# Two-chunk attention visits, two-bank PSUM tiles and a sliced second matmul in a kernel of blocked linear attention followed by a two-layer ELU network

## The chip, the cores and the metric

The kernel runs on one core of one Trainium2 chip. The metric is the device time of one execution in microseconds (us). A profiled execution also gives a span, from its first to its last instruction; here the span is about 1.8 us below the time.

## The reference, cut to what matters

For each of 4 sequences and 8 heads of width 64, attention runs over 768 positions in blocks, with a state per head that decays by a head's own lambda:

```python
intra = (qb @ kb.T * Dmask) @ vb                 # inside a block, masked by lam ** (i - j)
inter = (qb * lam_pow) @ kv_state                # from the blocks before
out_block = intra + inter
kv_state = lam_block * kv_state + (kb * rev_pow).T @ vb
# then, on x = the 3072 tokens x 512 features of out:
h = x @ w_in                                     # 512 -> 2048
g = where(h > 0, h, exp(min(h, 0)) - 1)          # ELU
y = g @ w_out                                    # 2048 -> 512
```

Both kernels use blocks of 128 positions. One block of one sequence with all 8 heads is a *chunk*; there are 24 chunks, six of each sequence. Four chunks (the same block of the four sequences) make a *tile* of 512 tokens. Chunks 0 to 3 feed tile 0, chunks 4 to 7 tile 1, and so on.

## The kernel before

Engines are called PE (matrix), DVE (vector), ACT (scalar), POOL (GpSimd) and SP (sync). A chunk goes through five stages, and the names of their PSUM tiles are the names in the profile: T (`psT`, 8 transposes of q and k), S (`psS`, 8 score matmuls, then DVE multiplies by the mask into `P`), O (`psO`, output, then DVE scales it into `xt`), U (`psU`, the state's update) and the state's own update `st`. A tile's first layer is 16 steps of four matmuls (`psH`), each followed by `e` and `r` on ACT and `g` on DVE; the second layer is 64 matmuls (`psM`).

```python
def att_U(g):                       # one chunk
    ...                             # 8 matmuls into pu
    for hh in range(2):
        r = slice(hh * 64, (hh + 1) * 64)
        if c == 0:
            nc.scalar.copy(out=new[r, :, r], in_=pu[r]); continue
        for hp in range(HP):        # HP = 4: eight pieces of 64 x 64 per chunk
            h = 2 * hp + hh
            nc.vector.scalar_tensor_tensor(
                out=new[r, hp, r], in0=old[r, hp, r], scalar=up[r, h : h + 1],
                in1=pu[r, hp, :], op0=ALU.mult, op1=ALU.add)
# ... cut: T, S, O of one chunk each, in one-bank PSUM tiles ...

# the first tile: T(j), S(j-1), O(j-2) of its four chunks
# then one step per first-layer block; one chunk's stages are placed among them:
for t in range(1, NT):
    for i in range(TS[t]):
        base = (t - 1) * NF + ([1, 4, 8, 11][i] if t == 1 else [-2, 2, 6, 10][i])
        at(base, att_T, g);     at(base, att_kd, g)
        at(base + 2, att_S, g); at(base + 2, att_U, g)
        at(base + 3, att_O, g)
for t in range(NT):
    for n in range(NF):             # NF = 16
        er = mm1(t, n)              # 4 matmuls, exp and relu
        for f in slots.get(t * NF + n, []): f()
        elu(t, n, *er)
        if t > 0: ...               # 4 matmuls of the second layer of tile t - 1
```

All loads but lambda's are issued on POOL's software queue and cast to 16 bits on the way. So a step holds eight 512-column matmuls, except in tile 0, whose steps hold four: its second layer runs wholly beside tile 1.

## Time and profile before

| | before |
|---|---|
| time, median of the first 3 runs | 249.97 us (249.71 to 250.82) |
| span of the profiled run (its time was 248.66) | 246.9 us |
| first PE work | 5.00 us |
| first `psH` of tile 0 | 23.15 us |
| first `psH` of tile 1 | 63.35 us |
| last matmul ends | 242.84 us |

The page of the kernel before: the span, the busy time of each engine, then rows that cut the span into 40 slices of about 6.2 us (busy share in tenths; PEclk is the granted clock of PE in tenths).

```profile
span 246.9 us, 4269 instructions
PE 217.1 (88%) x1664; PEld 107.1 (43%) x1664; DVE 163.9 (66%) x353; ACT 137.7 (56%) x265; POOL 51.7 (21%) x55
...
PE   0375748866999999999999999999999999999993
...
DVE  6347493999979877977977897787447644444210
...
PEclk9999995999999999999999999999999999999999
```

The average of 88% hides two regimes. From the eleventh slice on, PE is full; before, it is often idle, and DVE is nearly full from the eighth slice (43 us) to the eleventh (to 68 us). In the seventh slice (37.05 to 43.22 us) the granted clock of PE is 0.52. Only what happens before 65 us looks as if better overlap could save it.

Three of its groups of instructions (count, total busy us, mean ns of one, idle time before them):

```profile
L329 DVE SCALAR_TENSOR_TENSOR g<-e,r 128x512 f16<-128x512 f32 x96 | 65.8, 688 | 47.7 <-ACT r L325 47.2
...
L247 DVE TENSOR_TENSOR P<-psS,mask 128x512 f16<-128x512 f32 x48 | 30.8, 683 | 2.2 <-PE psS L242 1.9
L273 DVE SCALAR_TENSOR_TENSOR st<-st,up,psU 64x64 f16<-64x64 f16 x128 | 27.8, 279 | 0.2
```

The state's 128 small pieces cost 279 ns for 64 columns, where a `g` does 512 columns in 688 ns: the small ones are mostly fixed cost (an estimate: 448 columns more cost 409 ns, so 64 columns would be some 58 of the 279 ns).

What PE waited for (us in all, times, longest), and the busy times in a stretch of tile 0 (window, length, then busy us of PE, PEld, DVE, ACT, POOL, then clock, DMA share, GB/s):

```profile
PE psT L207 <- DMA qn<-in_q_dram: 8.4, 3, 5.0
PE psU L262 <- DVE st L273: 3.7, 1, 3.7
PE psU L262 <- ACT kT L216: 2.9, 2, 1.7
```

```profile
23.15:63.35 40.20, 28.27 (x264) 14.38 (x264) 31.20 (x72) 21.95 (x44) 20.56 (x20) 0.92 2.27 176
42.00:62.00 20.00, 15.18 (x159) 7.83 (x158) 18.80 (x46) 10.80 (x21) 10.27 (x9) 0.97 2.78 162
```

The second of these windows shows DVE busy for 18.8 of 20 us: there DVE sets the pace, with the four chunks of tile 1 beside tile 0's ELUs. The timeline of PE (start us, length us, what, and in brackets the idle time before it and what ended it) shows the start of tile 0, then one steady stretch of four steps:

```profile
23.15 3.25 PE L315 MATMUL psH<-xt,wi 128*128 128x512 f16 x8 [0.78 <-DVE xt L299]
...
84.70 1.04 PE L341 MATMUL psM<-wo,g 128*128 128x512 f16 x4
...
89.47 1.03 PE L315 MATMUL psH<-xt,wi 128*128 128x512 f16 x4
90.43 0.40 PE L242 MATMUL psS<-qT,kT 64*128 64x128 f16 x8
90.76 0.32 PE L262 MATMUL psU<-vn,kd 128*64 128x64 f16 x8
91.01 1.04 PE L341 MATMUL psM<-wo,g 128*128 128x512 f16 x4
...
93.41 1.04 PE L341 MATMUL psM<-wo,g 128*128 128x512 f16 x4
```

The first eight matmuls take 0.41 us each where four take 0.86 us in the steady part (0.216 each); the granted clock reads 1.00 there, and 0.50 at 40.34 us, where eight take 3.20 us. From 84.70 to 93.41 is one period with one chunk: 8.71 us, of which the 32 big matmuls are 6.91 and one chunk's visit is 1.8.

### The profile page before, as it was taken

The numbers are of one execution on the slowest core, as the hardware profiler recorded it, in microseconds if no ns is written. First come the engines' busy times: TensorE is split into PE (matmuls) and PEld (weight loads), VectorE is DVE, ScalarE is ACT, GpSimd is POOL, SyncE is SP. The second block draws the span as 40 slices with busy tenths as digits, with TensorE's granted clock in tenths as the row PEclk, the third lists the DMA queues.
The fourth block names the chain that finished last, engine by engine and source line by source line (L and its number), as shares of the span: only waits on it lengthen the run. The fifth ranks groups of instructions, "written<-read, shape, count | busy, mean of one in ns | idle before, by whom it ended". The sixth has DMA issues, their size and how long they took to land.

```text
span 246.9 us, 4269 instructions
## 1 busy us (share of the span) xinstructions
PE 217.1 (88%) x1664; PEld 107.1 (43%) x1664; DVE 163.9 (66%) x353; ACT 137.7 (56%) x265; POOL 51.7 (21%) x55
## 2 busy tenths in 40 slices
PE   0375748866999999999999999999999999999993
PEld 0243324433445445545544554454454444444441
DVE  6347493999979877977977897787447644444210
ACT  4510735645675576476566656755765757666200
POOL 8996455166551031000000000000000000000000
PEclk9999995999999999999999999999999999999999
DMA  8999999999999979110110111011101101111212
GB/s 51 140 170 171 181 190 206 177 156 147 148 145 170 131 50 123 44 45 0 45 44 9 37 42 43 2 44 45 42 3 42 42 1 45 42 42 42 79 51 85
DMA packets 83924, 20.20 MB, mean 82 GB/s; under 512 B 76096, under 2 KB 80960, under 8 KB 83904
## 3 DMA queue, kind: packets, MB, share of 16 engines
q0 software_dynamic: 80160, 13.63, 87.0%
q1 hardware_dynamic: 3600, 6.17, 6.9%
q8 instruction: 13, 0.21, 0.4%
q10 hardware_dynamic: 144, 0.13, 0.2%
q14 instruction: 7, 0.06, 0.1%
HBM read 27.27 MB, written 6.29 MB: 136 GB/s over the span
## 4 chain that ended last, share of the span: by engine, by line
PE 78%; DVE 12%; DMA 3%; POOL 3%; ACT 2%; issue 1%; POOLq 0%; DVEq 0%
PE psM L341 35%; PE psH L315 31%; PE psT L207 3%; DVE P L247 3%; DMA kn<-in_k_dram 3%; PE psO L286 3%; DVE st L273 3%; DVE g L329 3%; PE psS L242 2%; PE psU L262 2%; DVE xt L299 2%; PE psO L293 2%; POOL qn L73 1%; DVE r L323 1%; DVE kd L223 1%
## 5 line engine op out<-in xcount | busy, mean ns | idle before, releaser
L315 PE MATMUL psH<-xt,wi 128*128 128x512 f16 x384 | 101.2, 388 | 2.5 <-DVE xt L299 1.4
L329 DVE SCALAR_TENSOR_TENSOR g<-e,r 128x512 f16<-128x512 f32 x96 | 65.8, 688 | 47.7 <-ACT r L325 47.2
L320 ACT ACTIVATE e<-psH 128x512 f32<-128x512 f32 x96 | 57.4, 598 | 71.8 <-PE psH L315 65.9
L341 PE MATMUL psM<-wo,g 128*128 128x512 f16 x384 | 96.3, 380 | 0.0
L315 PEld LDWEIGHTS <-wi 128*128 128x128 f16 x384 | 37.4, 100 | 47.9 <-issue 6.8
L325 ACT ACTIVATE r<-psH 128x512 f16<-128x512 f32 x91 | 53.9, 592 | 0.0
L341 PEld LDWEIGHTS <-g 128*128 128x128 f16 x384 | 34.3, 98 | 36.6
L247 DVE TENSOR_TENSOR P<-psS,mask 128x512 f16<-128x512 f32 x48 | 30.8, 683 | 2.2 <-PE psS L242 1.9
L273 DVE SCALAR_TENSOR_TENSOR st<-st,up,psU 64x64 f16<-64x64 f16 x128 | 27.8, 279 | 0.2
L207 PE MATMUL psT<-ident,qn 128*128 128x128 f16 x96 | 10.4, 237 | 10.7 <-DMA qn<-in_q_dram 8.4
L216 ACT COPY kT<-psT 128x512 f16<-128x512 f16 x24 | 14.6, 607 | 9.2 <-DVE qT L212 9.2
L299 DVE TENSOR_TENSOR xt<-psO,qs 128x512 f16<-128x512 f32 x24 | 16.5, 688 | 4.0 <-PE psO L293 2.9
L73 POOL DMA_DIRECT2D qn<-in_q_dram x13 | 14.7, 1131 | 17.5 <-PE psT L207 10.6
L286 PE MATMUL psO<-P,vn 128*64 128x128 f16 x192 | 15.2, 242 | 3.2 <-DVE xt L299 1.7
L73 POOL DMA_DIRECT2D vn<-in_v_dram x13 | 14.6, 1122 | 12.8 <-PE psO L293 7.7
L73 POOL DMA_DIRECT2D kn<-in_k_dram x13 | 14.6, 1123 | 8.0 <-DVE g L329 3.1
L286 PEld LDWEIGHTS <-vn 128*64 128x64 f16 x192 | 10.6, 119 | 11.6 <-issue 11.6
L214 ACT COPY qT<-psT 128x512 f16<-128x512 f16 x20 | 11.8, 591 | 5.7 <-PE psT L207 5.6
L223 DVE TENSOR_TENSOR kd<-kn,ks 128x512 f16<-128x512 f16 x20 | 13.7, 683 | 1.5 <-PE psU L262 1.4
L207 PEld LDWEIGHTS <-qn 128*128 128x128 f16 x96 | 7.6, 104 | 15.9 <-DMA qn<-in_q_dram 8.9
L207 PE MATMUL psT<-ident,kn 128*128 128x128 f16 x96 | 10.4, 238 | 2.7 <-DMA kn<-in_k_dram 2.7
L361 ACT COPY osb<-psM 128x512 f32<-128x512 f32 x12 | 7.1, 591 | 9.6 <-PE psM L341 9.6
(37 smaller groups left out, 90.8 us busy)
## 6 DMA issues: line engine op xcount, KB each, us to landing
out_dram<-osb SPq DMA_DIRECT2D x23, 256.0 KB, 2.0
qn<-in_q_dram POOLq DMA_DIRECT2D x11, 256.0 KB, 12.6
kn<-in_k_dram POOLq DMA_DIRECT2D x11, 256.0 KB, 12.4
vn<-in_v_dram POOLq DMA_DIRECT2D x11, 256.0 KB, 12.5
wo<-in_moe_w_out_dram POOLq DMA_DIRECT2D x4, 512.0 KB, 16.8
wi<-in_moe_w_in_dram POOLq DMA_DIRECT2D x2, 512.0 KB, 12.9
wi<-in_moe_w_in_dram POOLq DMA_DIRECT2D x3, 256.0 KB, 9.5
qn<-in_q_dram POOLq DMA_DIRECT2D x2, 128.0 KB, 4.0
```

Of the source, the lines that this page charges most:

```text
L73: nc.gpsimd.dma_start(out=dst, in_=src[b : b + n, :, rows].rearrange("b h p d -> p (b h) d"))
L207: nc.tensor.transpose(pt[:, j, hp, :], in_=nat[:, 2 * hp : 2 * hp + 2, :], identity=ident16[:])
L223: nc.vector.tensor_tensor(out=dst, in0=heads(kn, g), in1=ks[:].unsqueeze(2).broadcast_to([128, H, 64]), op=ALU.mult,)
L247: nc.vector.tensor_tensor(out=P[:, hh], in0=ss[hh][:], in1=mask[:, hh], op=ALU.mult)
L273: nc.vector.scalar_tensor_tensor(out=new[r, hp, r], in0=old[r, hp, r], scalar=up[r, h : h + 1], in1=pu[r, hp, :], op0=ALU.mult, op1=ALU.add,)
L286: nc.tensor.matmul(po[r, hp, :], lhsT=v_of(g, 2 * hp + hh), rhs=P[:, hh, hp, :], start=True, stop=(c == 0), skip_group_check=True,)
L299: nc.vector.tensor_tensor(out=xt[t][:, :, i * L : (i + 1) * L], in0=po[:], in1=qs[:], op=ALU.mult)
L315: nc.tensor.matmul(pH[:], lhsT=wi[:, kk, j * 128 : (j + 1) * 128], rhs=xt[t][:, kk, :], start=(kk == 0), stop=(kk == HP - 1),)
L320: nc.scalar.activation(e[:], pH[:], AF.Exp)
L325: nc.scalar.activation(r[:], pH[:], AF.Relu)
L329: nc.vector.scalar_tensor_tensor(out=gt[t][:, n, :], in0=e[:], scalar=-1.0, in1=r[:], op0=ALU.add, op1=ALU.min)
L341: nc.tensor.matmul(pm[:], lhsT=gt[t][:, n, i * L : (i + 1) * L], rhs=wo_t[wo_at[n][0]][:, wo_at[n][1], :], start=(n == 0), stop=(n == NF - 1),
```

## The change

The intent is to empty the time before 65 us. Six parts:

1. q, k, v of chunk 0 are loaded uncast on the hardware queues of SP and ACT; DVE casts q and k, ACT casts v.
2. Attention visits two chunks at once (T of two, S of two, then O and U of two), with PSUM tiles of two banks.
3. The state's update is one POOL multiply and one DVE add of 512 elements per half of the partitions and pair of chunks, in place of 16 pieces.
4. Tile 0's second layer starts in slices: one slice per step late in tile 0, then 16 steps without a first layer, the rest beside tile 1.
5. The order of the first four chunks is written out, with nine matmuls that only keep PE busy (`warm`).
6. The state's zeroes move from DVE to POOL; four ELUs of tile 0 move part of their work from ACT to DVE; the load buffers go from 6 to 12.

```diff
+    for w, src, e in (("q", q, nc.sync), ("k", k, nc.scalar), ("v", v, nc.sync)):
+        e.dma_start(out=first[w][:], in_=src[0, :, 0:L].rearrange("h p d -> p h d"))
-    NB = 6
+    NB = 12
 ...
+    for w, ts in (("q", qn), ("k", kn)):
+        nc.vector.tensor_copy(ts[0][:, 0:H, :], first[w][:])
 ...
+        nc.scalar.copy(vn[0][:, 0:H, :], first["v"][:])
 ...
+    def att_tmp(g, eng="p"):
+        for hh in range(2):
+            e.tensor_tensor(out=tmp[r], in0=old[r, :, :, r],
+                in1=up_p[r].unsqueeze(1).unsqueeze(3).broadcast_to([64, 2, HP, 64]), op=ALU.mult)
+    def att_st(g):
         for hh in range(2):
             if c == 0:
-                nc.scalar.copy(out=new[r, :, r], in_=pu[r])
-            for hp in range(HP):
-                nc.vector.scalar_tensor_tensor(out=new[r, hp, r], in0=old[r, hp, r], ...)
+                (nc.scalar.copy if hh else nc.vector.tensor_copy)(out=new[r, :, :, r], in_=pu[r])
+            else:
+                nc.vector.tensor_tensor(out=new[r, :, :, r], in0=tmps[g][r], in1=pu[r], op=ALU.add)
 ...
+    def visit(g, s0, s1, s2, s3=None):
+        at(s0, att_T, g, 2, "q"); at(s0, att_T, g, 2, "k")
+        ...
+        at(s1, att_S, g); at(s1, att_S, g + 1)
+        at(s1, att_mask, g); at(s1, att_mask, g + 1)
+        at(s2, att_tmp, g)
+        at(s2, att_O, g, 2); at(s2, att_U, g); at(s2, att_X, g, 2); at(s2, att_st, g)
+    for g, vs in [(4, (('A', 11), ('A', 13), ('A', 15))), (6, (('B', 7), ('B', 10), ('B', 13))),
+                  (8, ((1, 0), (1, 2), (1, 4))), (10, ((1, 8), (1, 10), (1, 12))), ...
+    steps = [(('A', 0), (0, 0), []), ...              # 'A': tile 0's first layer
+             (('A', 10), (0, 10), [(0, 0, 0), (0, 1, 0)]), ...   # with slices of its second
+             (('B', 0), None, []), ... (('B', 15), None, [(0, 0, 15), (0, 1, 15)]),
+             ((1, 0), (1, 0), [(0, 2, 0), (0, 2, 1)]), ...       # two per step beside tile 1
+             ((2, 0), (2, 0), [(1, 0, 0), (1, 0, 1), (1, 0, 2), (1, 0, 3)]), ...
```

(Marks of cuts: three dots. The names `A`, `B` are steps of tile 0 with and without a first layer.)

## The prediction

> **What bounds the kernel now.** The span is 246.9 us (timed runs about 3 us more). The timeline shows two regimes. From 64.9 us to its last matmul at 242.8 us PE never stops: four 512-column matmuls start every 0.86 us, one attention chunk adds 1.79 us (8.70 us per four steps, 6.91 of it matmuls); 4.05 us of copy and store follow. So counted, PE needs about 207 us in all; 246.9 - 207 - 4 leaves about 36 us of idle or half-rate PE, all before 65 us: 5.0 us until the first q lands; to 23.15 us loads and eviction chains of tile 0's four chunks; then DVE (busy 18.8 of the 20 us of window 42 to 62) holds tile 0, with tile 1's attention between its first matmuls. The list of waits shows PE waiting 8.4 us on q loads, 3.7 on st, 2.9 on kT. At 23.15 and 40.3 us eight first-layer matmuls take 3.2 us (0.41 each against 0.216)[...].
>
> **What the change does.**
> - Chunk 0 comes over hardware queues; the other loads issue 2.6 us earlier (three issues of 0.88). [...]k of chunks 2 and 3 landed at 14.7, I expect about 13. Adds two DVE casts of about 0.4 us, one ACT copy of 0.5.
> - State updates: DVE did 16 pieces (2 x 1.75 us) per pair of chunks; now two adds of 512 elements, about 0.6 us each. Saves about 2.2 us of DVE per pair, 17 us in all. The decay multiply goes to POOL, behind load issues.
> - Wider ops save only fixed cost: mask 1.28 to about 1.2 us per chunk.
> - Eight memsets (2.1 us) leave DVE; four ELUs of tile 0 move work from ACT to DVE.
> - Tile 0's first matmul runs with little attention in between; its second starts in slices, spread over tile 0, a phase without first matmul, and tile 1. PE work is unchanged but for nine warming matmuls.
>
> **Arithmetic.** Steady part: PE-bound, no gain. Head: first PE at about 4.5 us; first-layer matmul at about 18.5 (was 23.15). Up to tile 1's first matmul PE then has 13.8 (first layer) + 6.9 (half of tile 0's second) + 7.7 (updates, attention of tile 1) = 28.3 us; I add 1 us cold clock, 1.5 us DVE queueing (early steps need about 10.4 us of DVE against 8 of PE), 1.5 us mask and eviction waits in the phase without first matmul. Tile 1 begins at about 51 us. Loads agree: at the 170 to 200 GB/s of the profile's row, the last wo lands near 46 us. Remaining PE work 172.8 us, 0.5 us of stalls in tile 1, 4.05 tail: span 228, time **231 us**, range 226 to 238. Chances: faster 0.95, within 2% 0.04, slower 0.01.
>
> **What would show it.** Tile 0's first psH matmul at 18 to 19 us; tile 1's near 51; PE unbroken from about 60 us, same 0.86 us per four; DVE busy about 15 us lower; st below 12 us; the same 4 us end.
>
> **What would make it wrong.** Hardware loads of 256-byte rows slow the others, so tile 0 and the late wo slices wait. Two rotating two-bank buffers serialise T, S, O and U. DVE stalls on POOL's multiply, queued behind loads. Cold clock through tile 0. If all overlaps better than I add up, 226.

18.5 + 28.3 + 1 + 1.5 + 1.5 = 50.8, about 51, and 51 + 172.8 + 0.5 + 4.05 is about 228. The 1 us of cold clock (PE at half rate) and the two 1.5 us are allowances; each of the two slow stretches of eight matmuls in the kernel before lost about 1.5 us (3.2 - 8 x 0.216). The times for the adds and the copy on ACT fit what that kernel shows from start to start: 0.60 us for 512 columns back to back on DVE (94.58, 95.18, 95.78 us), 0.49 on ACT (84.24, 84.73); the time for the casts fits DVE's copies of `qT`, 0.42 us. From start to end, in the changed kernel, an add took 0.68 us, the two casts on DVE 0.43 and 0.79, the cast on ACT 0.60.

## The result, and the profile after

| | before | after | difference |
|---|---|---|---|
| time, median of 4 | 250.39 us (249.71 to 251.27) | 229.44 us (229.26 to 229.47) | -20.95 |
| span of the profiled run | 246.9 | 227.5 | -19.4 |
| first PE work | 5.00 | 7.27 | +2.27 |
| first `psH` of tile 0 | 23.15 | 20.79 | -2.36 |
| tile 0 to the first `psH` of tile 1 | 40.20 | 33.69 | -6.51 |
| from there to the end of the last matmul | 179.49 | 169.20 | -10.29 |
| tail | 4.06 | 3.82 | -0.24 |

The ratio is 0.916 (95% interval 0.9127 to 0.9193), faster. A ratio here is the mean time of one kernel's runs over the mean of the other's of the same rounds, so not quite the ratio of the medians that are quoted. Executions over 1.5% slower than the fastest of the same kernel are left out of the means. The profiled run of before was 1.7 us faster than its median, which is why the spans differ by less than the times.

The last two phases of the table must be read together. Of tile 0's 64 second-layer matmuls, 32 (32 x 0.216 = 6.9 us) moved from beside tile 1 into tile 0's phase. So tile 0's phase became 6.5 us shorter although it took in 6.9 us of PE work, and the later phase lost those 6.9 us and 3.4 us besides.

The page and the groups after:

```profile
span 227.5 us, 4119 instructions
PE 209.0 (92%) x1673; PEld 105.4 (46%) x1673; DVE 148.3 (65%) x193; ACT 135.9 (60%) x244; POOL 75.2 (33%) x75
...
PE   0488969989998999999999999999999999999993
...
DVE  2549885798876999997887667647537544534110
...
PEclk9999988999999999999999999999999999999999
...
L379 DVE SCALAR_TENSOR_TENSOR g<-e,r 128x512 f16<-128x512 f32 x92 | 68.6, 758 | 46.0 <-ACT r L368 45.4
...
L346 DVE TENSOR_TENSOR st<-tmp,psU 64x512 f16<-64x512 f32 x16 | 10.9, 681 | 2.0 <-POOL tmp L328 1.8
```

PE is at 80% or more from the third slice (11 us) on, but for the sixth (28 to 34 us), and full from the fourteenth. DVE lost 15.6 us of work. `st` fell from 27.8 to 10.9 us; but a `g`, the same instruction on the same shape, now takes 758 ns on average instead of 688. With shapes kept apart, the mask costs this after:

```profile
L256 DVE TENSOR_TENSOR P<-psS,mask 128x1024 f16<-128x1024 f32 x20 | 23.5, 1217 | 0.7 <-PE psS L244 0.4
```

This is 1217 ns a chunk for what were two instructions of 683 (1.28 us back to back). So twice the width takes 534 ns more; an estimate from these two means is that 149 of the 683 ns do not grow with the width.

The waits of PE, the window of tile 0 and PE's timeline after:

```profile
PE psT L210 <- DVE qn L162: 7.3, 1, 7.3
PE psS L244 <- ACT kT L221: 3.0, 4, 1.2
PE psH L359 <- ACT r L368: 2.3, 2, 1.8
```

```profile
20.79:54.48 33.69, 29.93 (x288) 15.08 (x288) 26.51 (x36) 19.60 (x35) 23.34 (x22) 0.95 1.90 176
```

```profile
7.27 0.61 PE L210 MATMUL psT<-ident,qn 128*128 128x128 f16 x4 [7.27 <-DVE qn L162]
...
20.79 2.75 PE L359 MATMUL psH<-xt,wi 128*128 128x512 f16 x12
...
31.86 1.02 PE L359 MATMUL psH<-xt,wi 128*128 128x512 f16 x4 [1.82 <-ACT r L368]
33.33 1.86 PE L359 MATMUL psH<-xt,wi 128*128 128x512 f16 x4 [0.45 <-ACT r L368]
...
99.76 0.61 PE L210 MATMUL psT<-ident,qn 128*128 128x128 f16 x8
...
104.20 0.62 PE L244 MATMUL psS<-qT,kT 64*128 64x128 f16 x16
104.76 1.04 PE L387 MATMUL psM<-wo,g 128*128 128x512 f16 x4
...
116.50 0.61 PE L210 MATMUL psT<-ident,qn 128*128 128x128 f16 x8
```

Four readings. PE's idle time in tile 0's phase fell from 40.20 - 28.27 = 11.9 us to 33.69 - 29.93 = 3.8. The first twelve `psH` run at the full rate (2.75 us for twelve, 0.23 each, against 3.25 for eight before, 0.41 each). The first PE work comes 2.3 us later than before. And the steady period of eight steps with two chunks is 116.50 - 99.76 = 16.74 us; less 13.82 for 64 big matmuls, a pair's visit costs 2.92 us, where two single visits cost 2 x (8.71 - 6.91) = 3.6: about 0.67 us saved per pair.

The late first work is a matter of loads. Issue to landing, in the first 22 us, before and then after (KB, then the median us):

```profile
qn<-in_q_dram POOLq DMA_DIRECT2D x2, 128.0 KB, 4.0
```

```profile
q_first<-in_q_dram SPq DMA_DIRECT2D x1, 256.0 KB, 5.6
```

The uncast load on the hardware queue landed 1.6 us later after its issue than the casting one, and a cast of 0.43 us follows. The two loads come from different kernels, though, and did not meet the same traffic: in the same 22 us of the changed kernel the 128 KB casting loads of q took 7.6 us (median of three; before, 4.0).

### The profile page after: what moved, and what is told of

Same layout as the page of the kernel before. It is cut to its first block, busy times and chain, and to the rows that moved or that the text cites. A ratio compares the mean times of both kernels' runs of the same rounds, so it can differ in the third digit from the quotient of the medians.

```text
span 227.5 us, 4119 instructions
## 1 busy us (share of the span) xinstructions
PE 209.0 (92%) x1673; PEld 105.4 (46%) x1673; DVE 148.3 (65%) x193; ACT 135.9 (60%) x244; POOL 75.2 (33%) x75
## 4 chain that ended last, share of the span: by engine, by line
PE 73%; DVE 10%; ACT 9%; issue 3%; DMA 2%; POOL 1%; SPq 0%; DVEq 0%; ACTq 0%
PE psM L387 33%; PE psH L359 29%; DVE P L256 5%; PE psT L210 4%; ACT e L364 3%; DMA q_first<-in_q_dram 2%; DVE g L379 2%; PE psO L269 2%; PE psS L244 2%; ACT r L368 2%; DVE xt L293 2%; PE psO L277 1%; ACT qT L221 1%; ACT kT L221 1%; POOL tmp L328 1%
## 5 line engine op out<-in xcount | busy, mean ns | idle before, releaser
L359 PE MATMUL psH<-xt,wi 128*128 128x512 f16 x384 | 98.8, 382 | 2.4 <-ACT r L368 2.3
L379 DVE SCALAR_TENSOR_TENSOR g<-e,r 128x512 f16<-128x512 f32 x92 | 68.6, 758 | 46.0 <-ACT r L368 45.4
L256 DVE TENSOR_TENSOR P<-psS,mask 128x1024 f16<-128x1024 f32 (+1 forms) x28 | 28.7, 1065 | 4.1 <-PE psS L244 3.8
L328 POOL TENSOR_TENSOR tmp<-st,up_p 64x512 f32<-64x512 f16 x16 | 20.2, 1261 | 22.6 <-DVE st L346 21.6
L293 DVE TENSOR_TENSOR xt<-psO,qs 128x1024 f16<-128x1024 f32 (+2 forms) x15 | 14.9, 1004 | 6.3 <-PE psO L277 5.4
L221 ACT COPY qT<-psT 128x1024 f16<-128x1024 f16 (+1 forms) x14 | 12.6, 896 | 7.1 <-PE psT L210 7.1
L269 PE MATMUL psO<-P,vn 128*64 128x128 f16 x192 | 12.6, 227 | 1.3 <-DVE P L256 0.8
L221 ACT COPY kT<-psT 128x1024 f16<-128x1024 f16 (+1 forms) x14 | 12.8, 916 | 0.0
L231 DVE TENSOR_TENSOR kd<-kn,ks 128x1024 f16<-128x1024 f16 x10 | 12.3, 1229 | 0.0
L346 DVE TENSOR_TENSOR st<-tmp,psU 64x512 f16<-64x512 f32 x16 | 10.9, 681 | 2.0 <-POOL tmp L328 1.8
```

The source lines that it names most:

```text
L221: nc.scalar.copy(out=dst[:], in_=pt[:, j])
L256: nc.vector.tensor_tensor(out=P[:, :, c], in0=s[:, :, c], in1=mask[:, :, c], op=ALU.mult)
L269: nc.tensor.matmul(po[r, i, hp, :], lhsT=v_of(g + i, 2 * hp + hh), rhs=P[:, hh, hp, :], start=True, stop=(c == 0), skip_group_check=True,)
L293: nc.vector.tensor_tensor(out=xt[t][:, c, i * L : (i + n) * L].rearrange("p h (n l) -> p n h l", n=n), in0=po[:, :, c], in1=qs[:, c].unsqu ...
L328: e.tensor_tensor(out=tmp[r], in0=old[r, :, :, r], in1=up_p[r].unsqueeze(1).unsqueeze(3).broadcast_to([64, 2, HP, 64]), op=ALU.mult,)
L359: nc.tensor.matmul(pH[:], lhsT=wi[:, kk, j * 128 : (j + 1) * 128], rhs=xt[t][:, kk, :], start=(kk == 0), stop=(kk == HP - 1),)
```

## The experiments

All twelve kernels gave correct results. Those of one batch ran on one chip; differences in us are given within a batch where possible. Two kernels that came out equal to the changed one (no warming, 229.56 us; six buffers, 229.25 us) serve as its stand-ins in the second and third batch. In the first and the fourth batch no such stand-in ran, and 229.44 us is used for the first. The batches ran on different chips; the kernel before, which ran in each, had medians of 249.39, 249.61, 249.13 and 249.14 us.

The profile of each kernel is one execution. Eight kernels have the same instructions as the change up to the first `psH` (the change, e2, e3, e5, e6, e7, e9, e11), and it began anywhere from 20.65 to 21.39 us. The change, e2 and e5 have the same instructions up to tile 2, and tile 1 began at 54.48, 53.56 and 53.77 us. So a shift of less than about 0.9 us between two profiles proves nothing by itself.

| run | batch | median us | lowest to highest | ratio to before |
|---|---|---|---|---|
| the change | - | 229.44 | 229.26 to 229.47 | 0.9160 |
| e1_sw_first | 1 | 231.40 | 230.49 to 232.74 | 0.9289 |
| e2_split_visits | 1 | 237.26 | 237.17 to 237.29 | 0.9519 |
| e3_st_act | 1 | 229.19 | 228.49 to 229.63 | 0.9186 |
| e4_no_slices | 1 | 232.36 | 231.56 to 234.09 | 0.9332 |
| e5_split_later | 2 | 233.24 | 233.01 to 233.40 | 0.9341 |
| e6_st_act_tmp_early | 2 | 227.45 | 227.38 to 227.76 | 0.9113 |
| e7_st_act_tmp_dve | 2 | 229.00 | 228.37 to 229.06 | 0.9166 |
| e8_no_warm | 2 | 229.56 | 229.22 to 230.15 | 0.9197 |
| e9_narrow_st | 3 | 231.45 | 230.63 to 232.64 | 0.9290 |
| e10_v_sw_best | 3 | 226.00 | 225.93 to 226.60 | 0.9073 |
| e11_nb6 | 3 | 229.25 | 228.85 to 229.68 | 0.9199 |
| e12_vcast_dve | 4 | 226.80 | 225.79 to 227.21 | 0.9098 |

### e1_sw_first: chunk 0 back on the casting software queue

```diff
-    first = {...}; hardware loads of q, k, v; casts on DVE and ACT
-    LOADS = [(1, 1, 'q'), (1, 1, 'k'), ...
+    LOADS = [(0, 1, 'q'), (0, 1, 'k'), (0, 1, 'v'), (1, 1, 'q'), (1, 1, 'k'), ...
```

> The changed kernel with chunk 0 of q, k, v taken back to the casting software queue (first three issues there), without the two DVE casts and the ACT cast; all else as changed. Theory: the hardware loads land late (q at 6.8 us, three 256 KB loads in flight beside the software ones), so undoing them brings the first PE work from 7.3 back to about 5.0 us, but the other nine loads issue 2.6 us later; net, tile 0's first psH within 1 us of the changed kernel's 20.8 us, total 228 to 231 us. Rival (intent of the change): the hardware loads pay because the rest comes earlier; undone, psH starts at 22 us or later and the total is 231.5 us or more.

Measured: 231.40 us, about 2 us slower than the change, between the theory's range and the rival's. PE's first work came at 4.91 us instead of 7.27, but the first `psH` at 20.25 instead of 20.79 (0.4 us before the earliest of the eight kernels above) and tile 1's at 53.78 instead of 54.48 (within the scatter). So the late first work cost little: the head is bound by what follows it. The loss came after tile 1's start, 1.9 us of it in the profiled run. There DVE waited 4.6 us for POOL's multiply instead of 1.8. This is taken up after e8.

### e2_split_visits and e5_split_later: the same stages, one chunk at a time

In the visits from tile 2 on, T, S, O and U of the two chunks go to neighbouring steps instead of one. The wide copies, masks and state updates stay. e2 left S where it was; e5 moves S and O one step later.

```diff
-    at(s0, att_T, g, 2, ...);  at(s1, att_S, g); at(s1, att_S, g + 1);  at(s2, att_O, g, 2); at(s2, att_U, g)
+    at(s0, att_Tn, g, 0);  at(nxt(s0), att_Tn, g, 1);  copies of qT, kT after the second
+    at(s1, att_S, g);      at(nxt(s1), att_S, g + 1)
+    s2 = nxt(s2)                       # e5 also: s1, s2 = nxt(s1), nxt(s2) before all this
+    at(s2, att_On, g, 0); at(s2, att_Un, g, 0);  at(nxt(s2), att_On, g, 1); at(nxt(s2), att_Un, g, 1)
```

> The changed kernel, but in tiles 2 to 4 PE visits one chunk at a time (T, S, and O with U of the two chunks each in steps of their own); DVE, ACT and POOL instructions and PSUM tiles stay two-chunk. Theory: part of the gain is PE time itself: each switch between full-array and half-array matmuls costs about 0.1 to 0.2 us, and a pair of chunks cost 3.58 us before and 2.92 us after; splitting six visits gives back 0.6 us each, total 229.4 + 3.6 = about 233 us, and DVE busy unchanged. Rival: the batching helps only by fewer DVE and ACT instructions, and PE time per chunk did not change; then the total stays within 0.5 us of 229.4.

Measured: 237.26 us, 4 us above what was expected. (The 0.1 to 0.2 us per switch is an estimate. Of one way in the trace of before shows 0.10: four `psH` take 0.96 us ahead of `psS`, from 89.47, and 0.86 otherwise. A pair saves four switches, and its 0.66 us are 0.16 for each.) PE waited ten times for the copy of kT (8.1 us in all; 3.0 in the changed kernel), because the copies now come a step later and S did not move. The period of eight steps was 18.06 us, 1.32 longer, 0.82 of it this wait. So e2 mixed two things, and e5 was made to take the wait away.

> The split of the visits of tiles 2 to 4 again, with S and O one step later each, because in the first split PE waited 0.8 us per visit for the late kT copy (8.1 us in all), which hid what was asked. Theory: with that wait gone only the switches between full-array and half-array matmuls are left, about 0.5 us per visit (18.06 us per eight steps there against 16.74, less 0.82 of wait), six visits: 229.4 + 3 = 232 to 233 us, with kT waits near the 3.0 us of the changed kernel. Rival: splitting costs PE nothing by itself: 229 to 230 us.

Measured: 233.24 us, 3.7 us above its stand-in, just above what was expected. The wait for kT was back to 3.2 us. PE's timeline of e5, one period:

```profile
117.85 0.39 PE L323 MATMUL psT<-ident,qn 128*128 128x128 f16 x4
...
135.03 0.39 PE L323 MATMUL psT<-ident,qn 128*128 128x128 f16 x4
```

The period is 17.18 us against 16.74, so 0.44 us per visit without any wait; six visits make 2.6 us. The span grew by 4.0. The rest is waits of PE's first layer for `xt`, none of which the changed kernel has:

```profile
PE psH L407 <- DVE xt L293: 0.8, 3, 0.4
```

The periods from 100.28 and from 135.03, which hold one such wait each, are 17.57 and 17.58 us, 0.4 longer. e2, whose O comes a step earlier, has no such wait, so they come from e5's own later places, and of its 3.7 us about 2.6 belong to the splitting. Visiting in pairs thus saves time on PE itself, in the steady part, which the prediction held to be out of reach. The likeliest seat of it is what e5 doubles and the waits do not show: each time PE passes between 128-row and smaller matmuls, about 0.1 us is lost (0.96 us for four `psH` ahead of an S, 0.86 otherwise; 0.86 too ahead of T, whose matmuls are 128*128 like those of `psH`). On the way out it is about as much: to the start of the next matmul 8 S take 0.33 us in e5 and 16 take 0.56 in the change, so 0.10 comes once per group; for O with U it is 0.70 and 1.27, so 0.13. In e5 the two extra groups of small matmuls, each with a way in and a way out, would make 0.4 of the 0.44 us. Why PE loses this time the traces do not show; that splitting costs it is measured.

### e4_no_slices: tile 0's second layer wholly beside tile 1

```diff
-    steps: 'A' with slices from step 10, 'B' without first layer, two per step beside tile 1
+    steps: 16 x (first layer of tile 0), then 16 x (first layer of t, 4 of the second of t - 1) for every t >= 1
-    visits of chunks 4 and 6 at ('A', 11, 13, 15), ('B', 7, 10, 13)
+    visits of chunks 4 and 6 at ('A', 6, 8, 10), ('A', 11, 13, 15); their loads earlier
```

> The changed kernel without slicing: tile 0's second matmul runs whole in tile 1, four matmuls a step as in the other tiles; no phase without first matmul; both visits of tile 1 in tile 0's steps (6, 8, 10 and 11, 13, 15), their loads before wo. Theory: the slices fill PE while tile 0 is held by DVE and evictions; without them tile 1 starts at about 51 us instead of 54.5 but has 6.9 us more to do: total about 233 us (231.5 to 235). Rival: the slices only move work and the phase without first matmul costs what it fills; then total 228 to 230.5 us.

Measured: 232.36 us, 3 us slower, as the theory said. The phase with few PE instructions per step now waits: once for kT, 3.7 us, and then the clock is cold:

```profile
37.48 3.59 PE L359 MATMUL psH<-xt,wi 128*128 128x512 f16 x8
```

Eight matmuls in 3.59 us are 0.43 to 0.45 each, and the page's granted clock is at five tenths in that slice (34.8 to 40.7 us). The two runs with a mean granted clock of 0.985 took 234.09 and 233.00 us, the two at 1.0 took 231.72 and 231.56: the cold clock costs this schedule about 1.9 us when it strikes, and it is 2.2 us slower than the change even without. So the kernel without slices is 2 to 4 us slower. What the slices alone are worth is not shown, because e4 also moves the visits of chunks 4 to 7 to just after the steps in which the first states are copied, and the 3.7 us wait comes from there: ACT's copies of q and k stood behind its half of those states, for which ACT idled 2.1 and 1.7 us until DVE had done the other half (the pairing that e3, below, removes). That the slices fill PE while tile 1's attention runs remains the likely reason. e4's profiled run is also the slowest of its four.

### e3_st_act: the first states are both copied by ACT

The largest wait of PE in tile 0 of the changed kernel, 1.82 us for `r` at 31.86, goes back to the copy of tile 0's first states, half of it on a busy DVE.

```diff
-    (nc.scalar.copy if hh else nc.vector.tensor_copy)(out=new[r, :, :, r], in_=pu[r])
+    nc.scalar.copy(out=new[r, :, :, r], in_=pu[r])
```

> The changed kernel with the first-row state copies of tile 0 (two halves of one tile, DVE then ACT) both on ACT. Theory: ACT waits there for DVE's copy of the other half (1.6 and 0.9 us of ACT idle), which ends in PE waiting 1.8 + 0.5 us for r at 30 to 33 us and then 3.4 us at half clock (1.7 us lost); with both on ACT the wait and the cold stretch go, total 226 to 227.5 us. Rival: the wait at 30 us comes from DVE being overloaded in the first eight steps (e and r buffers), and ACT gets more work; then the total stays within 0.7 us of 229.4, or is slower.

Measured: 229.19 us, no gain. The wait shrank to 0.27 us, no stretch of the first layer was cold (the page's granted clock is at nine tenths or more in every slice), and tile 1 began at 52.87 us, 1.6 us earlier (e6 and e7, which copy the states in the same way, began it at 53.21 and 53.26, all three before the 53.56 to 54.48 of the change, e2 and e5). But the rest took 1.9 us longer. DVE's waits in e3 name the taker:

```profile
DVE st L346 <- POOL tmp L328: 4.9, 4, 2.2
```

DVE waited 4.9 us for POOL's multiply, which is issued behind loads, against 1.8 in the changed kernel. The theory was half right: the wait went away, and the gain was given back in tile 1. POOL's multiplies come in pairs, one for each half of the partitions. The second pair starts almost at the same time in both kernels (first the change, then e3), although e3 came to tile 1 1.6 us earlier:

```profile
52.96 2.14 POOL L328 TENSOR_TENSOR tmp<-st,up_p 64x512 f32<-64x512 f16 x2
```

```profile
53.36 2.14 POOL L328 TENSOR_TENSOR tmp<-st,up_p 64x512 f32<-64x512 f16 x2
```

The cold stretch at 33 us (granted clock 0.50 from 33.33 to 36.00) cannot explain much either: the changed kernel's four runs had mean clocks of 0.992, 1.0, 0.998 and 0.993 and took 229.26, 229.41, 229.47 and 229.46 us.

### e6_st_act_tmp_early: the multiply is issued as soon as its state exists

```diff
 (e3, and)
-    at(s2, att_tmp, g)                  # same step as O and U, behind loads on POOL
+    if g < 8:
+        at(('A', 6 if g == 4 else 8), att_tmp, g)
 ...
     at(s2, att_st, g)
+    at(s2, att_tmp, g + 4)              # right after the state it reads
```

> Both first-row state copies on ACT (as before), and POOL's decay multiply issued as soon as the state it reads exists, ahead of the later loads in POOL's queue. Theory: the 1.6 us that the ACT copies gained before tile 1 were lost in tile 1, where DVE waited 4.9 us for the multiply, which stood behind loads that wait for older loads to land; with it ahead, those DVE waits fall under 1 us and the total is 226.5 to 228 us. Rival: tile 1 is held by the multiply's own running time beside DVE (DVE's g mean is 758 ns beside POOL work, 688 before), which this doesn't change: 229 us within 0.6.

Measured: 227.45 us, 2.1 us faster than its stand-in in the same batch, as expected. (Waits of loads for older loads do show: up to 1.6 us in the changed kernel, before POOL issued the next. For the longest halt of POOL ahead of e3's multiply, 3.1 us before the load at 50.24, the profile shows no releaser.) DVE no longer waits for POOL's multiply at all. The price shows in the group of `g`, 803 ns on average against 758. A part of it may come from an oversight: for chunks 20 to 23 `att_tmp(g + 4)` asks for a multiply that nothing reads, so this kernel, e10 and e12 run 20 multiplies, not 16.

```profile
L379 DVE SCALAR_TENSOR_TENSOR g<-e,r 128x512 f16<-128x512 f32 x92 | 72.6, 803 | 40.1 <-ACT r L368 39.8
```

### e7_st_act_tmp_dve: the multiply on DVE

```diff
 (e3, and)
-    def att_tmp(g, eng="p"):
+    def att_tmp(g, eng="v"):
```

> Both first-row state copies on ACT, and the decay multiply on DVE instead of POOL. Theory (POOL helps little): DVE does 16 more ops of about 0.6 us (10 us), but loses the waits for POOL (4.9 us) and the slower g beside POOL (about 70 ns on 92, 6 us); DVE busy changes by less than 6 us, and the total is 228 to 230 us. Rival (the offload matters): DVE is short in tile 1 by all of it, total 231 us or more.

Measured: 229.00 us, as the theory said. The multiply takes 682 ns on DVE from start to end, 10.9 us for the 16. `g` is back at 689 ns, so it is POOL's multiply that stretches it; but DVE carries the multiply itself and PE once waits 1.8 us for `xt`. In the changed kernel one sees both engines in the same place. DVE's and POOL's timelines of the changed kernel:

```profile
112.01 2.13 DVE L379 SCALAR_TENSOR_TENSOR g<-e,r 128x512 f16<-128x512 f32 x2
```

```profile
112.06 2.99 POOL L328 TENSOR_TENSOR tmp<-st,up_p 64x512 f32<-64x512 f16 x2 [13.37 <-DVE st L346]
```

Two `g` take 2.13 us beside two multiplies, 1.4 without (2 x 0.69). What the two engines contend for the traces do not show. Behind the loads, POOL's multiply is no better than DVE's (229.19 us in e3, in another batch, and 229.00 here); issued early it is (e6, 227.45 us in the same batch).

### e8_no_warm: without the nine warming matmuls

```diff
     def warm(k, n=512):
-        if k <= 0:
-            return
+        return
```

> The changed kernel without its nine warming matmuls. Theory: [...]without them the first first-layer matmuls take 0.43 us each for about 3.4 us, as before the change (first eight in 3.2 us); psH then starts about 0.5 us earlier but tile 0 ends 1 to 1.5 us later; total 229.5 to 231 us. Rival: eviction and DVE hold tile 0, so the clock there doesn't matter and the total is within 0.4 us of 229.4 or lower.

Measured: 229.56 us, the same as the change. PE's timeline of e8:

```profile
19.67 4.44 PE L359 MATMUL psH<-xt,wi 128*128 128x512 f16 x12 [0.62 <-DVE xt L293]
```

The first layer begins 1.1 us earlier and takes 1.7 us longer (4.44 against 2.75). With the warming matmuls the first twelve `psH` run at 0.23 us each, without them at 0.37 on average, but nothing of it is left in the time. Tile 1 began at 53.76 us, 0.7 earlier than in the change, which is within the scatter, and from there DVE waited longer for POOL's multiply (3.1 us against 1.8), as in e1 and e3. So e8 shows that they don't pay in this schedule, not what they would be worth where POOL doesn't hold tile 1.

**The state's multiply explains the loose end of e1.** Each kernel's rest of the span after tile 1's first `psH`, beside DVE's total wait for POOL's multiply:

| | the change | e1 | e3 | e8 | e11 | e6 | e10 | e12 |
|---|---|---|---|---|---|---|---|---|
| wait of DVE for `tmp`, us | 1.8 | 4.6 | 4.9 | 3.1 | 0.3 | none | none | none |
| tile 1's first `psH` to the end, us | 173.0 | 174.9 | 174.9 | 173.8 | 172.0 | 172.4 | 172.4 | 172.4 |

The rest follows the wait, roughly 0.5 us for each us. An earlier tile 1 runs into POOL, which is still issuing loads, and gives its gain back: in the change, e3, e8 and e11 POOL's second and third pair of multiplies start at 52.8 to 53.4 and 64.0 to 65.2 us, though tile 1 begins anywhere from 52.87 to 55.38, and the spans end within 0.4 us of each other. In e1, with three more loads on POOL, they start at 54.1 and 65.8, and the span is 1.2 us longer. For e3 this was tested (e6 takes the wait away and keeps the gain); for e1 it is read from the same pattern, not tested.

### e9_narrow_st: the state in 16 pieces again

```diff
     def att_tmp(g, eng="p"):
+        return                          # no multiply on POOL
 ...
-    nc.vector.tensor_tensor(out=new[r, :, :, r], in0=tmps[g][r], in1=pu[r], op=ALU.add)
+    for i in range(2):
+        for hp in range(HP):
+            nc.vector.scalar_tensor_tensor(out=new[r, i, hp, r], in0=old[r, i, hp, r],
+                scalar=up_p[r, hp : hp + 1], in1=pu[r, i, hp, :], op0=ALU.mult, op1=ALU.add)
```

> The changed kernel with its state updates in 16 pieces of 64x64 per pair on DVE, as before the change; no multiply on POOL. Theory: with DVE the engine that holds tile 0's end and tile 1, the wide update is a main part of what shortened them: DVE per pair 3.5 us instead of 1.4, about 2 us on each of the visits of chunks 4 to 11, part of it hidden: total 231.5 to 234 us. Rival: as with the multiply on DVE (about 0 effect) there is slack for it: 228.5 to 230.5 us.

Measured: 231.45 us, 2.2 us above its stand-in, at the lower edge of the theory. `st` took 26.6 us in 128 pieces of 286 ns, `g` was back at 688 ns, and PE waited 2.5 us for `P` instead of 0.8. The 15.7 us more of `st` and the 6.7 us less of `g` make DVE 9.0 us busier (157.3 against 148.3), and that is worth about 2 us of time in this schedule; the rest was slack.

### e10_v_sw_best: e6, v of chunk 0 on the software queue, constants later

```diff
 (e6, and)
-    hardware loads of q, k, v;  nc.scalar.copy(vn[0][:, 0:H, :], first["v"][:])
+    hardware loads of q, k;  LOADS = [(1, 1, 'q'), (1, 1, 'k'), (0, 1, 'v'), (1, 1, 'v'), ...
-    ks, up_p before T(1)
+    ks, up_p after T(3)
```

> The run with POOL's multiply ahead, and besides: v of chunk 0 taken from the hardware queue to the casting software queue (third issue; no ACT cast), and two small constants computed after the fourth transpose. Theory: [...]with two hardware loads instead of three, q lands at about 6 us instead of 6.8 and the first psH comes 0.5 to 1 us earlier: total 226.3 to 227.2 us. Rival: the chain of copies and masks after the landing sets psH, not the landing: 227.4 us within 0.4.

Measured: 226.00 us, the fastest of all and 0.3 us below the expected range, 3.25 us under its stand-in and 0.9073 of before. The mechanism that had been named, earlier landing of q and k, was mostly wrong: q landed 5.3 us after its issue instead of 5.6 and k 4.4 instead of 4.9, the first PE work moved only from 7.27 to 7.11 us, while the first `psH` moved from 20.79 to 19.29 (e6: 21.33, at the late end of the scatter).

### e11_nb6: six load buffers

```diff
-    NB = 12
+    NB = 6
```

> The changed kernel with 6 instead of 12 buffers of q, k, v, so that late loads wait for a buffer again, as before the change. Theory: nothing waits for those loads before tile 2, but POOL's multiply stands behind them in its queue; total within 1 us of 229.4, DVE's wait for the multiply (1.8 us) longer. Rival: twelve buffers were needed for the loads themselves: 231 us or more, with PE waiting on loads.

Measured: 229.25 us, as expected; but DVE's wait for the multiply became shorter (0.3 us), not longer. The twelve buffers add nothing to the time.

### e12_vcast_dve: what part of e10's head gain is ACT's queue?

```diff
 (e6, ks and up_p after T(3), and)
-    nc.scalar.copy(vn[0][:, 0:H, :], first["v"][:])
+    nc.vector.tensor_copy(vn[0][:, 0:H, :], first["v"][:])
```

> The run with POOL's multiply ahead (227.45 us), with all three hardware loads of chunk 0 kept as in the change; only the ACT queue of the head is shortened: the cast of v goes to DVE, which is idle then, and two small constants are computed after the fourth transpose. In the last run psH came 2.0 us earlier (19.3 for 21.3) though q's transposes started only 0.13 us earlier, so the landing was not the cause I had named. Theory now: the ACT queue between the first and second transposes (cast 0.6, two constants 0.5 us) delayed the chain; with it shortened but the landing unchanged, psH comes at 19.3 to 20 us and the total is 225.7 to 226.6 us. Rival: the third hardware load delays what lands after it (chunk 1, constants); then psH stays at 20.8 us or later and the total at 227 us or more.

Measured: 226.80 us (six runs, 225.79 to 227.21), just above the theory's range, just below the rival's. All six lie below e6's four (227.38 to 227.76). The first `psH` came at 20.11, 0.5 to 1.3 us before those of the eight kernels with the change's head, so relieving ACT in the first chunks does gain. How much of e10's lead is left for taking v off the hardware queue is not settled: 0.8 us lie between the `psH` of e12 and e10, no more than the scatter, and their times overlap. With v on the hardware queue, DVE's cast of k took 0.87 us instead of 0.41, that of q 0.43 instead of 0.57. Why, the traces do not show; that stays open.

## Why the prediction was right or wrong

The time (231 us, 226 to 238) held: 229.44. The sum inside it held less well. In spans:

| term | predicted | measured | error |
|---|---|---|---|
| tile 1's first `psH` | 51 | 54.48 | 3.5 too early |
| PE work from there, with 0.5 of stalls | 173.3 | 169.20 | 4.1 too much |
| tail | 4.05 | 3.82 | 0.2 too much |
| span | 228 | 227.5 | |

- **"First PE at about 4.5 us" was wrong.** It was 7.27: the hardware load landed 5.6 us after issue and is followed by a cast. The first q of the kernel before landed 1.6 us sooner through the casting software queue, with other traffic; beside the hardware loads, the changed kernel's own casting loads of q took 7.6 us (4.6 in e1, which has no hardware loads of q, k, v). So this doesn't decide which queue is faster, only that the move didn't bring q earlier. In e1 the first `psH` came 0.4 to 1.1 us earlier than in the kernels with the change's head, so little of the 2.3 us lay on the path.
- **"First-layer matmul at about 18.5" was wrong by 2.3 us**, and "tile 1 begins at about 51" by 3.5. The order of magnitude of the saved stalls was right: 11.9 us of idle PE became 3.8. Of the 3.5, 2.3 are the late start and 1.2 the phase itself (33.69 us against 51 - 18.5). What had been missed is that the cast of v and the late constants, both on ACT, sit on the path of the first four chunks: e12, which relieves ACT of them, has its first `psH` at 20.11. e10 began tile 1 at 51.65, but it also has e6's copies and order, and e6 alone began it at 53.21.
- **"Steady part: PE-bound, no gain" is the step that failed.** PE-bound was right, no gain was not. It treated PE work as fixed; a pair's visit costs about 0.67 us less than two visits, and e5, which splits six of them again, gives back 0.44 us each time even where nothing waits (2.6 us in all). That the total came so near was luck: this term, 4.1 us too much, hid the 3.5 us by which tile 1 was put too early. The time has one more such error: 231 is the span of 228 and 3 us, but time and span of one and the same run differ by 1.8.
- **The list of what could go wrong.** "DVE stalls on POOL's multiply, queued behind loads" was right and is worth about 2 us (e6). The two-bank buffers did not serialise the stages: no wait for them is among PE's largest (one of 0.35 us at 46.44, until DVE had read `psO` into `xt`); those for kT (3.0 us, four times) are for data. The other loads did land later after issue beside the hardware loads (128 KB of q: 7.6 us, 4.6 in e1), without a gain in e1. A cold clock in the first layer came only in a stretch at 33 us (granted clock 0.50), and the run at a mean clock of 1.0 was no faster than the others. The warming matmuls, whose benefit was taken into the sum as a cold clock of only 1 us, gain nothing in this schedule (e8).
- **DVE's sums were right**: busy 15.6 us lower (15 predicted), `st` 10.9 (below 12), mask 1217 ns a chunk (about 1.2 us). The total is partly luck: that POOL's multiply would lengthen `g` by 6.4 us (92 x 70 ns) was not foreseen, and savings that were not counted (5.2 us of `r` and `qT` that left DVE, about 3 of wider `xt` and `kd`) made up for it. And little of it reached the time: e9, with 9.0 us more on DVE, is only 2.2 us slower.
- **"PE unbroken from about 60 us" was nearly right**: two waits, 0.64 us at 72.9 and 0.22 at 77.0, come later.

What the parts are worth, each undone alone: pairs instead of single visits 3.7 us (e5, 1.3 of it by waits of e5's own), slices with their places for the visits 3 (e4), wide state 2.2 (e9), the hardware loads 2 (e1, through the wait for POOL, not through the head), warming 0 (e8), buffers 0 (e11). These sum to about 11 of 21 us. The remainder, the new order of the first chunks, the zeroes, the wider copies, and what the parts give only together, was not split further. e3, and by the same pattern e1 and e8, also show that a small gain before tile 1 does not reach the time as long as POOL's multiply stands behind the loads; a part that works only there may be worth more in e6's order.

## What to carry to other kernels

When a matrix engine looks full, ask what it loses between instructions: visiting small matmuls in larger groups freed about 0.67 us per pair, which no busy share showed. A gain early in the kernel is kept only if the engines that follow it are ready: what e3 gained before tile 1 (1.6 us, and by the same pattern e1) was given back in a wait for POOL, and issuing POOL's multiply right after its input (e6) kept it. Before optimising the busiest vector instruction, look whether the engine is on the path where it runs: 9 us more of DVE work (e9) cost 2.
